# An attention kernel with two MoE layers behind it: a new order for the first two pairs of heads, zero matmuls in five early gaps, K's rounded part by VectorE, and one visit for a pair's product with V

## The chip, the cores and the metric

The kernel runs on one NeuronCore of a Trainium2 chip. The metric is the device time of one execution in microseconds (us). PE is the matmul engine (TensorE), DVE is VectorE, ACT is ScalarE, POOL is GpSimd, and SP is SyncE, which issues all DMAs of this kernel.

## The reference

Inputs are q, k and v of shape (4, 8, 576, 64), a gate s of shape (4, 8, 576), and two pairs of weight matrices (512 x 2048 and 2048 x 512).

```python
def _attn_ref(q, k, v, s):
    scores = scale * np.matmul(q, k.transpose(0, 1, 3, 2))
    cum = np.cumsum(np.maximum(s, 0.0), axis=-1)
    bias = -(cum[:, :, :, None] - cum[:, :, None, :])
    scores = np.where(causal, -1000000000.0, scores + np.minimum(bias, 0.0))
    scores = scores - np.max(scores, axis=-1, keepdims=True)
    attn = np.exp(scores)
    attn = attn / (np.sum(attn, axis=-1, keepdims=True) + 1e-09)
    return np.matmul(attn, v)

def _moe_ref(x, w_in, w_out):
    h = x @ w_in
    return (h - np.tanh(h)) @ w_out

def _moe2_ref(x, w_in, w_out):
    h = x @ w_in
    return (h * np.clip(h + 3.0, 0.0, 6.0) / 6.0) @ w_out

def reference(q, k, v, s, ...):
    x = attention out, transposed to (4 * 576, 8 * 64)
    return _moe2_ref(_moe_ref(x, ...), ...)
```

## The kernel before, in words

The 32 heads are taken as 16 pairs. Every float32 value is kept as a rounded high part (float32r) and a low part, the rest.

For one pair the work is this. SP loads q and k (tile tq). ACT copies the high part of q into Q (`q1`), and POOL subtracts it from q for the low part (`ql`). The high part of K exists twice: one copy beside the row of cumulated gates, for the row maxima (`kh`), and one in the second set of tiles, for the scores (`k2`), from which POOL makes the low part (`kl`). In pairs 0 and 1 `kh` is a cast on DVE and `k2` a copy on ACT. In pairs 2 to 15 `kh` is a copy on ACT, and `k2` is a DMA that copies `kh`'s result from tile K to tile K; the number `KDMA = 2` says from which pair on.

PE then makes one pass of score products just for the row maxima (`mx`, 11 matmuls of 66 rows for a pair), DVE reduces them (`rd`), negates, splits and transposes them (`mf`), and two small DMAs carry them through DRAM into two rows of Q (`mo`, `mi`). After that PE makes the scores themselves (`st`, four chunks a head, 30 matmuls a pair), ACT takes the exponential of each chunk (`ex`), and PE multiplies with V and with a column of ones (`pv`, 128x32 matmuls, 72 + 48 of them). `PVG` says in how many visits PE does this: two visits here, chunks 0 and 1 first, then chunks 2 and 3 and the sums. After the last pair the two MoE layers follow, which are matmuls with conversions of the weights beside them on ACT and DVE.

The order of the instructions on each engine is made by a planner in the kernel file: each operation has an engine, a duration, its predecessors and a priority (table `PRIO`), and a list schedule gives the order in which the program is written down. Each engine then runs its own list in order and waits by semaphores. POOL's operations that share a memory port with DVE are written to wait for the last such DVE operation ahead of them.

Ahead of the first real matmul PE runs 18 matmuls on a tile of zeros (`WARM`, line 1362 of the profile). `FILLS` names operations on PE ahead of which more zero matmuls (128x256, bf16) are put, into a PSUM bank that is idle there; 0.9 stands for 7 of them. Before, there are two such places, ahead of `mx1_0` (the maxima of head 1) and ahead of `st0_0` (the first scores of head 0), 14 matmuls in all.

Before the first pair there is preparation: `cum` (the cumulated gates, on DVE), masks and an identity on POOL (`prep_mask`, `prep_rest`, `prep_ident`), rows of ones in the tiles of pairs 1 to 3 (`prep_first`, two copies on ACT each, lines 369 and 370), and zero columns (`prep_pad`, POOL). The copies of ones are planned as POOL's but run on ACT.

Of the kernel before, what the change touches and what calls it, by code (L numbers as in the profile page):

```python
# [68 lines left out]
KDMA = 2  # L69
# [10 lines left out]
PRIO = {  # L80
# [3 lines left out]
}  # L84
# [170 lines left out]
def vec_us(n, ghz, fixed):  # L255
    return (n / ghz + fixed) / 1e3
# [3 lines left out]
def kernel(  # L260
# [10 lines left out]
    nc = tc.nc  # L271
# [123 lines left out]
    def prep_rest():  # L395
        nc.gpsimd.memset(maskB, 0.0)
        for o in (0, D):
            nc.gpsimd.affine_select(
                out=maskB[o : o + D, 512:S], in_=maskB[o : o + D, 512:S], pattern=[[-1, D]],
                compare_op=ALU.is_ge, fill=-1.0e30, base=0, channel_multiplier=1,  # L400
            )
        for m in zeroed:
            nc.gpsimd.memset(m, 0.0)
        nc.gpsimd.memset(ones, 1.0)
        nc.gpsimd.memset(ones[D:P, 1], 0.0)
# [21 lines left out]
    pr = plan.op("POOL", 1.4, prep_rest, [pma], prio=lead)  # L427
    pid = plan.op("POOL", 1.0, prep_ident, [pr], prio=lead + 1)
    prep = [pf0]
    for i in range(1, NS1):  # L430
        prep.append(plan.op("POOL", 2.6, lambda i=i: prep_first(i), [prep[-1] if i > 1 else pr], prio=lead + i, name=f"ones{i}"))
    pads = []
    for i in range(NS1):
        pads.append(plan.op("POOL", 0.3, lambda i=i: prep_pad(i), [prep[i], prep[0]] + prep[1 : 1 + (i == 0)] + pads[-1:], prio=lead + i + 0.5, name=f"pad{i}"))


# [9 lines left out]
    def heads(p):  # L446
# [6 lines left out]
        al = plan.op("V", 0.0, lambda: None, [alloc_prev[0]] + ([prep[p]] + (pads if p else []) if p < NS1 else []), [b1], t0, name=f"first{p}")  # L453
# [3 lines left out]
        for i, a in enumerate(parts):  # L457
# [23 lines left out]

            act, pool = vec_us(n * S, 1.2, 200), vec_us(n * S, 0.46, 60)
# [7 lines left out]
            oq1.append(plan.op("ACT", act + 0.22 * (p > 0), q1, [lq, al], [b1, tq], t + PRIO["q1"], name=f"q1_{p}"))  # L490
            if p >= KDMA:
                okh.append(plan.op("ACT", act, lambda a=a: nc.scalar.activation(r(b1)[1][0:64, a, 0:S], r(tq)[64:128, a], AF.Copy), [lk, al], [b1, tq], t + PRIO["kh"], name=f"kh{p}"))
                ok2.append(plan.dma(lambda a=a: move(r(b2)[1][64:128, a, 0:S], r(b1)[1][0:64, a, 0:S]), 147 * n, [okh[-1], a2], [b1, b2], t + PRIO["k2"], name=f"k2_{p}"))
            else:
              okh.append(plan.op("DVE", vec_us(n * S, 1.92, 150), kh, [lk, al], [b1, tq], t + PRIO["kh"], name=f"kh{p}", port=True))
              ok2.append(plan.op("ACT", act, k2, [lk, a2], [b2, tq], t + PRIO["k2"], name=f"k2_{p}"))
            oq2.append(plan.dma(q2, 147 * n, [oq1[-1], a2], [b1, b2], t + PRIO["q2"], name=f"q2_{p}"))
            oql.append(plan.op("POOL", pool, ql, [oq1[-1], a2] + first_mf[: p == 1], [b1, b2, tq], t + PRIO["ql"], name=f"ql{p}", port=True))
            okl.append(plan.op("POOL", pool, kl, [ok2[-1]], [b2, tq], t + PRIO["kl"] if p else lead + 3.5 + 0.1 * i, name=f"kl{p}", port=True))
# [15 lines left out]
        for c, (last, kind, tiles) in enumerate(MAXT[p > 0]):  # L515
# [38 lines left out]
            mm_mx[last].append(plan.op("DVE", us, rd, [om, pr, pma], [b, mt], u - PRIO["mx"] + PRIO["rd"], name=f"rd{n}"))  # L554
# [38 lines left out]
        lv = plan.dma(lambda: nc.sync.dma_start(r(vf).rearrange("p j a d -> p (j a d)"), v[p]), 338, first_mo[1:2] if p else first_mo[:1], [vf], t0 + PRIO["lv"], name=f"lv{p}")  # L593
        prep_done.extend(oq1 + okh + oql + okl + oq2 + ok2)
# [56 lines left out]
    def values_of(p, t0, got, vf, lv, xp, xb, bt):  # L651
# [776 lines left out]
```

## Time and profile before

| | us |
|---|---|
| median of three runs | 960.5 (960.0 to 960.62) |
| the profiled execution's own time | 959.44 |
| its span, first to last instruction | 957.6 |
| PE busy | 943.5, 99% of the span |
| DVE, ACT, POOL busy | 653.0, 467.7, 160.0 |
| mean granted clock of PE | 0.978 of full speed |

The attention part ends on PE at about 200 us of the span, the first MoE layer at about 600 us, the second with the end. Busy shares are averages over these parts, so the profile is read part by part. A busy PE need not be a PE at full speed: the granted clock stands beside it.

### The profile page before, as it was taken

What the parts mean: (1) busy time and instruction counts of PE and PEld (TensorE: products, weight loads), DVE (VectorE), ACT (ScalarE), POOL (GpSimd) and SP (SyncE); (2) the same over time, 40 slices, a digit from 0 to 9 for tenths busy, and PEclk for the clock granted to TensorE, in tenths of its full rate; (3) what the DMA queues carried; (4) which work ended last, traced back from release to release, by engine and by line L of the source; (5) the groups of instructions that cost most, each with busy time, mean ns of one, the idle gap of its engine ahead of it and who ended that gap; (6) DMA issues with size and microseconds to landing.
All of it is one profiled execution on the core that took longest, in us unless ns stands there. A gap on an engine that the chain in (4) does not pass through costs nothing.

```text
span 957.6 us, 17848 instructions
## 1 busy us (share of the span) xinstructions
PE 943.5 (99%) x7049; PEld 842.6 (88%) x7049; DVE 653.0 (68%) x1045; ACT 467.7 (49%) x720; POOL 160.0 (17%) x113
## 2 busy tenths in 40 slices
PE   7999999999999999999999999999999999999998
PEld 4787887888888888998888888999999999999997
DVE  5687576868988766775778723656776577764763
ACT  6478685755534443444344333444454444544441
POOL 6445755520000000002322322000000000000000
PEclk7599998999999999999999999999999999999999
DMA  4678988786336447545546681776786767877772
GB/s 113 177 178 217 257 205 230 171 316 196 130 131 220 173 158 267 192 178 199 197 159 242 204 274 38 248 222 208 249 314 222 233 200 256 302 232 223 208 224 98
DMA packets 71424, 197.86 MB, mean 207 GB/s; under 512 B 11696, under 2 KB 20496, under 8 KB 70060
## 3 DMA queue, kind: packets, MB, share of 16 engines
q1 hardware_dynamic: 71340, 196.72, 64.5%
q8 instruction: 55, 0.90, 0.4%
q14 instruction: 29, 0.24, 0.1%
HBM read 143.74 MB, written 44.09 MB: 196 GB/s over the span
## 4 chain that ended last, share of the span: by engine, by line
PE 93%; DVE 2%; DMA 1%; POOL 1%; ACT 1%; SPq 0%; issue 0%; DVEq 0%; POOLq 0%; ACTq 0%
PE bank L927 20%; PE bank L896 20%; PE pair L1264 19%; PE pair L1188 18%; PE bank L627 6%; PE bank L660 5%; PE bank L671 2%; PE bank L526 2%; PE wide L526 1%; DVE xr L535 1%; POOL K L480 1%; DMA tq<-in_k_dram 0%; DMA K<-cdram 0%; POOL Q L470 0%; DMA tq<-in_q_dram 0%
## 5 line engine op out<-in xcount | busy, mean ns | idle before, releaser
L927 PE MATMUL bank<-gg,w 128*128 128x512 f32 (+1 forms) x960 | 234.2, 368 | 0.2 <-ACT gg L915 0.2
L896 PE MATMUL bank<-xx,w 128*128 128x512 f32 (+1 forms) x960 | 233.3, 368 | 0.0
L896 PEld LDWEIGHTS bank<-xx,w 128*128 128x128 f32 x960 | 170.4, 188 | 30.4 <-DVE xx L883 0.2
L927 PEld LDWEIGHTS bank<-gg,w 128*128 128x128 f32 x960 | 170.1, 189 | 30.3 <-ACT gg L915 0.7
L907 ACT ACTIVATE g<-bank 128x512 f32<-128x512 f32 (+1 forms) x80 | 44.5, 556 | 153.1 <-PE bank L896 133.5
L1188 PE MATMUL pair<-op_w,w 128*128 128x384 f32 x648 | 118.0, 334 | 0.6 <-DVE f_w L1208 0.6
L1264 PE MATMUL pair<-w,op_W 128*128 128x256 f32 x918 | 115.1, 283 | 0.0
L1188 PEld LDWEIGHTS pair<-op_w,w 128*128 128x128 f32 x648 | 112.5, 188 | 1.2 <-DVE f_w L1208 0.9
L1264 PEld LDWEIGHTS pair<-w,op_W 128*128 128x128 f32 x918 | 112.8, 192 | 0.0
L917 POOL TENSOR_TENSOR gg<-g,gg 128x512 fp32r<-128x512 f32 x32 | 47.7, 1492 | 344.4 <-ACT gg L915 302.7
L911 DVE TENSOR_TENSOR g<-bank,g 128x512 f32<-128x512 f32 (+1 forms) x80 | 50.8, 636 | 64.7 <-ACT g L907 64.1
L535 DVE CUSTOM_DVE_ANT_0 xr<-bank,xr 128x512 bf16<-128x512 f32 (+3 forms) x96 | 48.9, 509 | 36.3 <-PE bank L526 26.6
L630 ACT ACTIVATE pt<-bank 128x512 f32<-128x512 f32 (+2 forms) x128 | 60.3, 504 | 19.9 <-PE bank L627 15.4
L627 PE MATMUL bank<-Q,K 128*128 128x320 f32 (+9 forms) x384 | 69.1, 326 | 0.6 <-POOL K L480 0.5
L915 ACT ACTIVATE gg<-g 128x512 fp32r<-128x512 f32 (+1 forms) x80 | 46.9, 587 | 40.0 <-DVE g L911 31.7
L627 PEld LDWEIGHTS bank<-Q,K 128*128 128x128 f32 (+3 forms) x384 | 60.0, 197 | 6.0 <-issue 1.6
L660 PE MATMUL bank<-pt,vf 128*32 128x192 f32 (+3 forms) x1152 | 52.0, 330 | 0.0
L470 POOL TENSOR_TENSOR Q<-tq,Q 64x1152 fp32r<-64x1152 f32 (+1 forms) x17 | 43.3, 2548 | 41.6 <-DVE xr L571 13.9
L480 POOL TENSOR_TENSOR K<-tq,K 64x1152 fp32r<-64x1152 f32 (+1 forms) x17 | 43.5, 2560 | 26.3 <-DVE xr L571 9.7
L660 PEld LDWEIGHTS bank<-pt,vf 128*32 128x32 f32 x1152 | 32.5, 114 | 15.1 <-ACT pt L630 3.1
L1264 PE MATMUL pair<-w,op_B 128*128 128x256 f32 x342 | 44.1, 283 | 0.0
L1264 PEld LDWEIGHTS pair<-w,op_B 128*128 128x128 f32 x342 | 42.5, 192 | 0.0
(316 smaller groups left out, 1340.1 us busy)
## 6 DMA issues: line engine op xcount, KB each, us to landing
w<-wdram SPq DMA_DIRECT2D x149, 512.0 KB
wdram<-cv SPq DMA_DIRECT2D x56, 512.0 KB
raw_c<-in_w_dram SPq DMA_DIRECT2D x11, 1024.0 KB
raw_b<-in_w_dram SPq DMA_DIRECT2D x11, 1024.0 KB
raw_a<-in_w_dram SPq DMA_DIRECT2D x12, 512.0 KB
vf<-in_v_dram SPq DMA_DIRECT2D x16, 330.0 KB
rb<-rdram SPq DMA_DIRECT2D x8, 576.0 KB
xdram<-xb SPq DMA_DIRECT2D x16, 288.0 KB
```

The costliest lines, as they stand in the source:

```text
L480: return nc.gpsimd.tensor_sub(x[0:64, a, 0:S], r(tq)[64:128, a], f32(x)[64:128, a, 0:S])
L535: nc.vector.tensor_tensor_reduce(out=junk[0:rr, 0:w], in0=r(b)[0:rr, col : col + w], in1=maskB[:, 0:w] if hh < 0 else maskA[0:rr, m0 : m0 ...
L627: nc.tensor.matmul(o, w, x, start=(i == 0), stop=(i == len(mms) - 1), skip_group_check=True)
L630: nc.scalar.activation(r(pt), r(b)[:, 0 : CW[c]], AF.Exp, scale=0.125)
L660: nc.tensor.matmul(r((wide_b, rest_b)[far])[32 * i : 32 * i + 32, oc : oc + n], r(vf)[:, j, hh, d0 : d0 + 32], r(pts[hh][c])[:, col : col ...
L896: nc.tensor.matmul(r(ps)[:, 0:w], wt[:, c, :], x(c)[:, 0:w], start=(part == 0 and c == 0), stop=(part == 2 and c == NCC - 1),)
L911: nc.vector.tensor_sub(x, r(ps)[:, 0:w], x)
L915: gho = plan.op("ACT", vec_us(w, 1.2, 205), lambda: nc.scalar.activation(r(gh)[:, 0:w], r(g)[:, 0:w], AF.Copy), [m, to_gg], [g, gh], base)
L917: glo = plan.op("DVE" if beside else "POOL", vec_us(w, 0.96, 155) if beside else vec_us(w, 0.44, 160), lambda: (nc.vector if beside else n ...
L927: nc.tensor.matmul(r(acc[e])[:, 0:w], a[:, es], bb[:, 0:w], start=f, stop=l)
L1188: nc.tensor.matmul(bank(k)[:, l], w[hw][:, l, kc], r(x)[:, hx, kc], start=(i in (1, 5, 2) and j == 0 and kc == 0), stop=(j == 2 and kc == ...
L1264: nc.tensor.matmul(r(c[k])[:, m * 256 : (m + 1) * 256], r(x)[:, hx, l, m * P : (m + 1) * P], w[hw][:, l], start=(i == order[chain_first[k] ...
```

## The change

Five things are edited.

1. The preparation is planned anew: the copies of ones are planned as ACT's and come later (pairs 1 and 2 behind pair 0's copies, pair 3 behind pair 1's), and POOL's mask for the last key block and the column of ones move to the end of the preparation (`prep_late`).
2. The table `PRIO` has other numbers, and early operations of pair 0 have fixed early places (`early`). Pair 1's maxima now stand ahead of head 0's scores.
3. `FILLS` names five places: 19 zero matmuls ahead of `mx1_0`, 4 ahead of `mx2_1`, 13 ahead of `st0_0`, 22 ahead of `mx4_1`, 13 ahead of `pv1_3`; 71 in all.
4. `KDMA = ()`: in every pair `kh` is a cast on DVE and `k2` a copy on ACT.
5. `PVG = ((0, 1, 2, 3),)`: all of a pair's product with V in one visit.

```diff
-FILLS = {"mx1_0": 0.9, "st0_0": 0.9}
+FILLS = {"mx1_0": 2.2, "mx2_1": 0.5, "st0_0": 1.6, "mx4_1": 2.6, "pv1_3": 1.6}
-PVG = ((0, 1), (2, 3))
+PVG = ((0, 1, 2, 3),)
-KDMA = 2
+KDMA = ()
...
     def prep_rest():
+        for m in zeroed:
+            nc.gpsimd.memset(m, 0.0)
+
+    def prep_late():
         nc.gpsimd.memset(maskB, 0.0)
...
-    for i in range(1, NS1):
-        prep.append(plan.op("POOL", 2.6, lambda i=i: prep_first(i), [prep[-1] if i > 1 else pr], prio=lead + i, name=f"ones{i}"))
+    def ones_of(i):
+        after = [prep[i // 3], pma, k2s[0]] if i < 3 else [prep[1], k2s[1]]
+        prep.append(plan.op("ACT", 2.4, lambda: prep_first(i), after, prio=lead + 4 + i, name=f"ones{i}"))
...
-            if p >= KDMA:
+            if p in KDMA:
                 okh.append(plan.op("ACT", act, lambda a=a: nc.scalar.activation(r(b1)[1][0:64, a, 0:S], r(tq)[64:128, a], AF.Copy), [lk, al], [b1, tq], t + PRIO["kh"], name=f"kh{p}"))
                 ok2.append(plan.dma(lambda a=a: move(r(b2)[1][64:128, a, 0:S], r(b1)[1][0:64, a, 0:S]), 147 * n, [okh[-1], a2], [b1, b2], t + PRIO["k2"], name=f"k2_{p}"))
             else:
               okh.append(plan.op("DVE", vec_us(n * S, 1.92, 150), kh, [lk, al], [b1, tq], t + PRIO["kh"], name=f"kh{p}", port=True))
-              ok2.append(plan.op("ACT", act, k2, [lk, a2], [b2, tq], t + PRIO["k2"], name=f"k2_{p}"))
+              ok2.append(plan.op("ACT", act, k2, [lk, a2], [b2, tq], early(t + PRIO["k2"], 1.05), name=f"k2_{p}"))
```

What this does to the order is shown at three places. The first is ACT at its start, before. Tiles Q_0 and K_0 belong to pair 0, Q_1, K_1 and Q_2 to pairs 1 and 2; L462 is `q1`, L476 is `k2`, L369 and L370 are the copies of ones.

```order
L423 ACTIVATE rb<-rb 32x576
L462 ACTIVATE Q_0_96<-tq 64x576
L476 ACTIVATE K_0_109<-tq 64x576
L369 ACTIVATE Q_1_99<-Q_0_96 4x1280
L370 ACTIVATE K_1_100<-Q_0_96 4x2x576
L462 ACTIVATE Q_0_96<-tq 64x576
L476 ACTIVATE K_0_109<-tq 64x576
```

The same place of the change; L466 and L480 are now `q1` and `k2`.

```order
L425 ACTIVATE rb<-rb 32x576
L466 ACTIVATE Q_0_96<-tq 64x576
L480 ACTIVATE K_0_109<-tq 64x576
L466 ACTIVATE Q_0_96<-tq 64x576
L480 ACTIVATE K_0_109<-tq 64x576
L369 ACTIVATE Q_1_99<-Q_0_96 4x1280
L370 ACTIVATE K_1_100<-Q_0_96 4x2x576
```

The second half of pair 0's q and k is now copied ahead of the ones. The second place is PE between the maxima of head 1 (K_0, Q_0 into bank_71) and the first scores, before; L526 is `mx`, L1347 a zero matmul and its weights, L627 `st`.

```order
L526 MATMUL bank_71<-K_0_97,Q_0_96 128x128
L1347 LDWEIGHTS xr
L1347 MATMUL bank_72<-xr 128x256
...
L627 MATMUL bank_72<-Q_0_108,K_0_109 128x256
L627 MATMUL bank_72<-Q_0_96,K_0_97 128x256
```

The same place of the change; L531 is `mx`, L1355 a zero matmul, L633 `st`, and K_1, Q_1 are pair 1's.

```order
L531 MATMUL bank_71<-K_0_97,Q_0_96 128x128
L1355 LDWEIGHTS xr
L1355 MATMUL bank_72<-xr 128x256
...
L531 MATMUL bank_72<-K_1_100,Q_1_99 128x512
L531 MATMUL bank_73<-K_1_100,Q_1_99 128x512
...
L1355 MATMUL bank_70<-xr 128x256
...
L633 MATMUL bank_70<-Q_0_108,K_0_109 128x256
```

Pair 1's maxima, eleven matmuls, moved from behind head 0's scores to ahead of them, with 4 zero matmuls ahead of them and 13 behind. The third place is DVE at the end of pair 1's maxima, in the change; L540 is `rd`, L569 to L576 are `mf`, L477 is `kh`, here of pair 2.

```order
L540 ISA xr<-wide,xr 128x384
L540 ISA xr 128x1
L569 COPY xr<-xr 64x1
L572 TENSOR_SCALAR xr<-xr 128x10
L573 SCALAR_TENSOR_TENSOR xr<-xr 128x10
L576 STREAM_TRANSPOSE xr<-xr 128x32
L477 CAST K_2_103<-tq 64x2x576
L540 ISA xr<-bank_65,xr 128x512
```

Before, there is no such cast from pair 2 on; ACT had this copy, and SP a DMA behind it, as these rows of SP show (K_2 is pair 2's, K_0_109 the second tile).

```order
L279 DMA K_0_97<-cdram 2x2x576
L279 DMA K_0_109<-K_2_103 64x2x576
L279 DMA Q_0_108<-Q_2_102 64x2x576
L279 DMA Q_1_99<-mdram 2x40x32
```

The row in the middle with K on both sides is gone from SP's list in the change, in 14 pairs; the cast on DVE is new in 14 pairs, right behind the transpose of the maxima.

## Rows read from the trace of the kernel before

**Rows 1.** The page: granted clock in 40 slices, and the chain by engine.

```profile
PEclk7599998999999999999999999999999999999999
PE 93%; DVE 2%; DMA 1%; POOL 1%; ACT 1%; SPq 0%; issue 0%; DVEq 0%; POOLq 0%; ACTq 0%
```

**Rows 2.** Windows: stretch, length, busy by engine (count), PE clock, DMA share, GB/s.

```profile
10.40:44.54 34.14, 30.18 (x167) 22.75 (x171) 21.41 (x78) 18.97 (x26) 14.30 (x19) 0.50 0.64 164
153.76:160.60 6.84, 6.84 (x40) 5.23 (x42) 2.04 (x8) 3.84 (x7) 6.18 (x3) 0.50 0.54 182
```

**Rows 3.** Timeline of PE at the start: start, length, group, idle before it.

```profile
11.70 1.14 PE L526 MATMUL wide<-K,Q 66*128 66x384 f32 x3 [3.48 <-POOL Q L375]
13.39 1.72 PE L1347 MATMUL bank<-xr 128*128 128x256 bf16 x7
16.73 1.14 PE L526 MATMUL wide<-K,Q 66*128 66x384 f32 x3 [1.62 <-DMA K<-rb]
20.50 0.58 PE L627 MATMUL bank<-Q,K 68*128 68x256 f32 x1 [0.15 <-DMA Q<-mdram]
57.09 1.07 PE L627 MATMUL bank<-Q,K 128*128 128x320 f32 x6
```

**Rows 4.** Timeline of SP's DMA queue at the start.

```profile
4.84 4.11 SPq L279 DMA_DIRECT2D Q<-Q  x2
9.07 1.23 SPq L279 DMA_DIRECT2D K<-rb  x2
```

**Rows 5.** Timeline of ACT at the start.

```profile
4.84 0.68 ACT L476 ACTIVATE K<-tq 64x576 fp32r<-64x576 f32 x1
7.76 0.68 ACT L462 ACTIVATE Q<-tq 64x576 fp32r<-64x576 f32 x1
```

**Rows 6.** Timeline of DVE: maxima of heads 0 and 1, `kh` of pair 1, `mf` of pair 5.

```profile
17.90 0.56 DVE L535 CUSTOM_DVE_ANT_0 xr<-wide,xr 128x384 bf16<-128x384 f32 x1 [1.14 <-PE wide L526]
21.69 0.75 DVE L473 CAST K<-tq 64x1152 fp32r<-64x1152 f32 x1
25.27 0.69 DVE L535 CUSTOM_DVE_ANT_0 xr<-bank,xr 128x512 bf16<-128x512 f32 x1 [2.82 <-PE bank L526]
31.32 0.15 DVE L564 COPY xr<-xr 64x1 f32<-64x1 f32 x1
32.05 0.65 DVE L535 CUSTOM_DVE_ANT_0 xr<-bank,xr 128x512 bf16<-128x512 f32 x1
54.70 1.83 DVE L567 TENSOR_SCALAR xr<-xr 128x10 fp32r<-128x10 f32 x1
```

**Rows 7.** Timeline of PE: a pair at full clock with one visit, to the next pair.

```profile
117.25 0.73 PE L526 MATMUL bank<-K,Q 66*128 66x512 f32 x2
119.16 0.46 PE L627 MATMUL bank<-Q,K 128*128 128x256 f32 x2
123.14 2.92 PE L660 MATMUL bank<-pt,vf 128*32 128x256 f32 x72
127.39 0.73 PE L526 MATMUL bank<-K,Q 66*128 66x512 f32 x2
```

**Rows 8.** The chain that ended last: four product visits of chunks 0 and 1.

```profile
83.29 1.11 PE bank L660 x24
93.78 1.11 PE bank L660 x24
144.67 1.11 PE bank L660 x24
159.39 1.72 PE bank L660 x24
```

**Rows 9.** Waits of 57 to 200 us: who for whom, total, times, longest.

```profile
PE wide L526 <- ACT K L492: 0.7, 1, 0.7
PE bank L627 <- POOL K L480: 0.5, 2, 0.3
```

**Rows 10.** Windows: the sum of six stretches, 48 to 192 us.

```profile
sum 144.00, PE 142.84 PEld 117.16 DVE 104.96 ACT 103.49 POOL 81.65; mean PE 23.81 PEld 19.53 DVE 17.49 ACT 17.25 POOL 13.61
```

More of the change, by code (lines that the diff above doesn't have):

```diff
@@ L401, in prep_rest @@
             )
-        for m in zeroed:
-            nc.gpsimd.memset(m, 0.0)
         nc.gpsimd.memset(ones, 1.0)
@@ L426 @@
     pma = plan.op("POOL", 2.0, prep_mask, prio=lead)
-    pr = plan.op("POOL", 1.4, prep_rest, [pma], prio=lead)
+    pr = plan.op("POOL", 0.4, prep_rest, [pma], prio=lead)
     pid = plan.op("POOL", 1.0, prep_ident, [pr], prio=lead + 1)
-    prep = [pf0]
-    for i in range(1, NS1):
-        prep.append(plan.op("POOL", 2.6, lambda i=i: prep_first(i), [prep[-1] if i > 1 else pr], prio=lead + i, name=f"ones{i}"))
-    pads = []
-    for i in range(NS1):
-        pads.append(plan.op("POOL", 0.3, lambda i=i: prep_pad(i), [prep[i], prep[0]] + prep[1 : 1 + (i == 0)] + pads[-1:], prio=lead + i + 0.5, name=f"pad{i}"))
+    pl = plan.op("POOL", 2.7, prep_late, [pid], prio=lead + 4, name="late")
+    prep, pads, k2s = [pf0], [None], []
+    def ones_of(i):
+        after = [prep[i // 3], pma, k2s[0]] if i < 3 else [prep[1], k2s[1]]
+        prep.append(plan.op("ACT", 2.4, lambda: prep_first(i), after, prio=lead + 4 + i, name=f"ones{i}"))
+        if i == 2:
+            pads[0] = plan.op("POOL", 0.3, lambda: prep_pad(0), [prep[1], prep[2], pl], prio=lead + 5, name="pad0")
+        pads.append(plan.op("POOL", 0.3, lambda: prep_pad(i), [prep[i], pl], prio=lead + 5 + i, name=f"pad{i}"))
     T = PRIO["T"]
@@ L451, in heads @@
         parts = [slice(0, 1), slice(1, 2)] if p == 0 else [slice(0, 2)]
-        al = plan.op("V", 0.0, lambda: None, [alloc_prev[0]] + ([prep[p]] + (pads if p else []) if p < NS1 else []), [b1], t0, name=f"first{p}")
+        al = plan.op("V", 0.0, lambda: None, [alloc_prev[0]] + ([prep[p], pads[p]] if p < NS1 else [pads[0]]), [b1], t0, name=f"first{p}")
         a2 = plan.op("V", 0.0, lambda: None, [alloc_prev[1]], [b2], t0, name=f"second{p}")
@@ L480, in kl @@
                 return nc.gpsimd.tensor_sub(x[0:64, a, 0:S], r(tq)[64:128, a], f32(x)[64:128, a, 0:S])
+            early = (lambda x, y: x if p else lead + y + 0.1 * i)
             act, pool = vec_us(n * S, 1.2, 200), vec_us(n * S, 0.46, 60)
@@ L489, in heads @@
             ) for x in range(2))
-            oq1.append(plan.op("ACT", act + 0.22 * (p > 0), q1, [lq, al], [b1, tq], t + PRIO["q1"], name=f"q1_{p}"))
-            if p >= KDMA:
+            oq1.append(plan.op("ACT", act + 0.22 * (p > 0), q1, [lq, al], [b1, tq], early(t + PRIO["q1"], 1), name=f"q1_{p}"))
+            if p in KDMA:
                 okh.append(plan.op("ACT", act, lambda a=a: nc.scalar.activation(r(b1)[1][0:64, a, 0:S], r(tq)[64:128, a], AF.Copy), [lk, al], [b1, tq], t + PRIO["kh"], name=f"kh{p}"))
@@ L495, in heads @@
               okh.append(plan.op("DVE", vec_us(n * S, 1.92, 150), kh, [lk, al], [b1, tq], t + PRIO["kh"], name=f"kh{p}", port=True))
-              ok2.append(plan.op("ACT", act, k2, [lk, a2], [b2, tq], t + PRIO["k2"], name=f"k2_{p}"))
+              ok2.append(plan.op("ACT", act, k2, [lk, a2], [b2, tq], early(t + PRIO["k2"], 1.05), name=f"k2_{p}"))
             oq2.append(plan.dma(q2, 147 * n, [oq1[-1], a2], [b1, b2], t + PRIO["q2"], name=f"q2_{p}"))
-            oql.append(plan.op("POOL", pool, ql, [oq1[-1], a2] + first_mf[: p == 1], [b1, b2, tq], t + PRIO["ql"], name=f"ql{p}", port=True))
-            okl.append(plan.op("POOL", pool, kl, [ok2[-1]], [b2, tq], t + PRIO["kl"] if p else lead + 3.5 + 0.1 * i, name=f"kl{p}", port=True))
+            oql.append(plan.op("POOL", pool, ql, [oq1[-1], a2] + first_mf[: 2 * (p == 1)], [b1, b2, tq], early(t + PRIO["ql"], 2), name=f"ql{p}", port=True))
+            okl.append(plan.op("POOL", pool, kl, [ok2[-1]] + first_mf[: 2 * (p == 1)], [b2, tq], t + PRIO["kl"] if p else lead + 3.5 + 0.1 * i, name=f"kl{p}", port=True))
         def cu():
@@ L553, in heads @@
                 b.spare = 384
-            mm_mx[last].append(plan.op("DVE", us, rd, [om, pr, pma], [b, mt], u - PRIO["mx"] + PRIO["rd"], name=f"rd{n}"))
+            mm_mx[last].append(plan.op("DVE", us, rd, [om, pr, pma] + [pl] * any(t[0] < 0 for t in tiles), [b, mt], u - PRIO["mx"] + PRIO["rd"], name=f"rd{n}"))
         rd_done.extend(mm_mx[0] + mm_mx[1])
@@ L593, in heads @@
         lv = plan.dma(lambda: nc.sync.dma_start(r(vf).rearrange("p j a d -> p (j a d)"), v[p]), 338, first_mo[1:2] if p else first_mo[:1], [vf], t0 + PRIO["lv"], name=f"lv{p}")
+        k2s.append(ok2[-1])
         prep_done.extend(oq1 + okh + oql + okl + oq2 + ok2)
@@ L680, in values_of @@
             pvs.append(plan.op(
-                "PE", us, lambda cs=cs, last=last: turn_of(cs, last), [g[0][c] for g in got for c in cs] + [lv, pr] + pvs[-1:],
+                "PE", us, lambda cs=cs, last=last: turn_of(cs, last), [g[0][c] for g in got for c in cs] + [lv, pl] + pvs[-1:],
                 [vf, wide_b, rest_b] + [g[1][c] for g in got for c in (range(4) if last else cs)],
@@ L747 @@
     for p in range(NPR):
+        if 0 < p < NS1:
+            ones_of(p)
         heads(p)
```

6 rows, old and new, of the table PRIO are left out of this document.

## The prediction

> **What bounds the kernel now.** I read the page first. The chain that ended last lies on PE for 93% of the span [rows 1], so a change pays only by what it takes from PE's list: idle time, matmul time, or time at a lower clock. The line of the granted clock shows where the last is: 0.7 and 0.5 of full speed in the first two slices of 24 us, one slice of 0.8 later, full speed nearly everywhere else [rows 1]. The windows cut at the edges give two stretches at half speed, the lower of PE's two levels (1.2 against 2.4 GHz): 34.14 us from 10.40, and 6.84 us from 153.76 [rows 2].
>
> PE's timeline at the start shows what came ahead. PE stood idle for 3.48 us up to 11.70 [rows 3], and the clock fell inside that gap. In the 34 us that follow PE is busy for 30.18 [rows 2], yet the clock does not return until the end. The fills that stand there, 7 zero matmuls at 13.39 [rows 3] and as many ahead of the first scores, did not bring it back.
>
> Behind 60 us PE is hardly idle up to the last store, so time won in the attention part should come out at the end, unless DVE, which converts the MoE weights, falls behind.
>
> **The change, part by part.**
>
> *The start.* The wait at 11.70 is put down to POOL [rows 3], but PE's matmul there also waits for the copies of the gate sums into K, which SP issued from 9.07 to 10.30. They stood behind a DMA of Q that held SP's queue until 8.95 [rows 4], because that DMA waits for the second copy of q on ACT, which began at 7.76. ACT's copy before it ended at 5.52 [rows 5]; between them lay the ones of pair 1. In the new order the ones come behind. The copy starts 2.24 us sooner, and SP's list with it: first maxima at 9.46 instead of 11.70, idle 1.24 instead of 3.48. The maxima of head 1 waited for the same kind of DMA [rows 3], behind the same list, and come at 14.49 instead of 16.73.
>
> *The new order with its fills.* I walk it at full clock. A pair costs 1.91 us of maxima (117.25 to 119.16), 3.98 of scores and 4.25 of product in one visit [rows 7]. Seven zeros took 1.72 at half clock [rows 3]: 0.246 each, 0.123 at full. Head 1's maxima (the six like them at 11.70 took 1.69 at half clock [rows 3]; I take 0.95) and 4 zeros run to 15.9, pair 1's maxima to 17.8, 13 zeros to 19.4, head 0's scores to 21.4 (their last rows of Q, through the gap at 20.50 [rows 3], come 2.24 sooner, at 18.3), and 22 zeros to 24.1.
>
> Then PE must wait for DVE, since pair 2's maxima need `kh` of pair 2, and that cast stands behind all of pair 1's maxima. DVE starts head 1 at 17.90 less 2.24, that is 15.66, and needs 3.79 for it with its `mf` (to 21.69). Pair 1 needs 6.05 (25.27 to 31.32), `mf` 0.73, the cast 0.75 [rows 6]. Sum: 26.98. So about 2.9 us behind the 22 zeros PE is idle, and these zeros cost nothing unless they run at half clock.
>
> From 26.98: pair 2's maxima to 28.89, head 1's scores to 30.88, 13 zeros to 32.48, the product to 36.73, pair 3's maxima to 38.64, pair 1's scores to 42.62, pair 4's maxima to 44.53, product to 48.78, and the first chunk of head 4 (0.4) to 49.2. Before, PE got past this same work at 57.09 [rows 3]. **Term 1: 7.9 us.**
>
> *One visit for the product.* Of the pairs behind 57 us, eight do the product in two visits. Two first visits lie 10.49 us apart (83.29 to 93.78 [rows 8]), a pair with one visit takes 10.14 (117.25 to 127.39 [rows 7]): 0.35 a pair. The change waits for a pair's later exponentials inside the visit, where the matmuls of the first chunks cover it. **Term 2: 2.8 us** (lower bound 0.)
>
> *K's high part.* The second low stretch lies between the visits at 144.67 and 159.39 [rows 8]: 14.72 us for a pair that costs 10.49. It began behind a wait of 0.7 us of the maxima for ACT's copy of K [rows 9]. This operation goes to DVE, right behind the transpose, and its DMA goes; the scores twice waited for POOL's low part of K, 0.5 together [rows 9], which stood behind that DMA. **Term 3: 4.2 us** if the clock holds here, 0 if another gap takes the place; **term 4: 0.5.**
>
> *What DVE pays.* Fourteen casts of 0.75 [rows 6] are 10.5 us. In 48 to 192 us DVE is busy for 104.96 of 144 [rows 10], idle for 39. ACT's work stays the same (one copy in place of another), SP loses 14 issues. The upper bound is set by DVE standing behind POOL: a tiny operation on ten columns took 1.83 us, while its like at 31.32 and behind, the whole `mf` of four, took 0.73 [rows 6]. So a cast costs PE between nothing and 0.75 + 1.83 = 2.58. I take 1 us in total, because the idle time is almost four times the casts. The Trainium skill, page "SBUF — State Buffer", section "SBUF: two separate sides", says that DVE in a two-port mode and POOL hold one port pair exclusively for a whole instruction, the loser blocked; the row of 1.83 us agrees. By that rule each cast that meets POOL could wait for the rest of a POOL subtraction, and at worst the 1 us would be 36; that is the rival on DVE below.
>
> *What the clock takes back.* No row shows PE's clock with a gap of 1.24 us behind the 18 zeros, nor with 19 zeros after it. Behind 3.48 us of idle it fell; behind the 0.7 us of rows 9 it fell as well; the gaps of the new order (1.24 ahead of the maxima, 1.7 ahead of head 1's, 2.9 ahead of pair 2's) lie between or near these. So I count on one fall in the first 30 us, with the zeros bringing the clock back before pair 2's maxima: from nothing to the 8.0 worked out below, and I take 3, since the wait for DVE absorbs 2.9 of the delay.
>
> **The sum.** 7.9 + 2.8 + 4.2 + 0.5 = 15.4 won, 1 + 3 given back: 11.4. The profiled execution took 959.44 (span 957.6); the median of the runs is 960.5, 1.06 above it. On the median: 960.5 - 11.4 = 949.1. I predict **949.1 us**. With nothing given back it is 945.1.
>
> **The rivals.**
>
> 1. *The zeros run at half clock and are in the way* (0.19). The fall comes at the first gap and the fills, as the 14 before, do not lift it until those ahead of pair 2. Then, with the other work at most doubled: 9.46 + 1.69 + 4.67 of zeros = 15.8; head 1's maxima 17.5, 4 zeros 18.5, pair 1's maxima 22.3, 13 zeros 25.5, scores 29.5, 22 zeros 34.9, against 26.98: 8.0 us. With 1 for DVE: 954.1. For it speaks that 30.18 us of busy PE did not lift the clock [rows 2], against it that a run of 22 zeros is three times as long as any of the old fills. If it is not lifted before the first product, maxima, scores, 13 zeros and the product add up to 9.8 more, 964.
>
> 2. *DVE becomes the bound* (0.10, on the other side). The place is each pair's cast behind `mf`: if DVE has no room when it comes, everything behind it, the next maxima and with them PSUM banks that PE waits for, comes later by 0.75 to 2.58 a pair. Fully exposed at 2.58 this is 36 us: 948.1 + 36 = 984; at 1.2 a pair it is 965. It decides from 1.0 a pair on (14.3 us over 14 pairs, counted from 948.1, the sum without DVE's 1). For it speak the row of 1.83, against it the 39 us of idle.
>
> 3. *The gain is given back in the first MoE layer* (0.10). DVE carries 10.5 us more while attention is 11 us shorter: of 39 us idle some 17 are left, in pieces. If the weight conversions planned into attention slip behind its end, PE waits for weights there. At two thirds of the gain lost: 957.
>
> 4. *The clock does what it did* (0.06): fall at the first gap, return only with the first product, the second dip again from another gap. Then only the 2.24 us of the start and term 2 remain, less what cold zeros cost: about 959.5, no change that can be told.
>
> **Chances and range.** The forecast has 0.55. A run of this kernel tells about 0.2%, 1.9 us, from no change. Faster holds the forecast, rival 3, and most of rival 1: 0.80. Same: rival 4, a part of 1 and of 2: 0.10. Slower: most of 2 and the tail of 1: 0.10. The low end is everything won with nothing given back, 945.1, less half a microsecond for the 0.95 and 0.4 that I took; the high end is past rivals 1 and 3. Range 944.6 to 958.5, which leaves out rivals 2 and 4 and the tail of 1.
>
> **What would show it.** Right: the first maxima near 9.5 us of the span and head 1's near 14.5; the granted clock of the first two slices at 0.8 or more, and the 128x256 zeros near 0.12 us each; pair 2's maxima at 27 to 30 us, released by DVE; no slice below 0.9 behind 48 us; a pair in 10.1 to 10.3 us; the attention's end on PE near 189 us, not 200. Wrong: zeros at 0.21 us or more, with pair 2's maxima behind 32 us and following a zero matmul without a gap (rival 1); maxima on PE waiting for the cast of K, or casts of over 1.5 us (rival 2); PE idle behind 250 us with ACT or DVE as the releaser of weights (rival 3); a new gap of 0.5 us or more behind 60 us with a low clock after it, which would take term 3 away.

## The result, and the profile after

The changed kernel takes 950.95 us (median of four executions, 948.91 to 952.27), the kernel before in the same comparison 960.56 (960.0 to 962.55): ratio 0.9894, 95% interval 0.9869 to 0.992. The forecast was 949.1. In a second comparison with more executions, on another chip (the run `a_again` below), the changed kernel took 951.07 and the kernel before 956.41: 0.9939, interval 0.9916 to 0.9963. The changed kernel came out alike both times; the kernel before did not. Where it was run 17 to 31 times on a chip, its times fall into two groups, on that second chip 15 of 952.2 to 956.4 us (mean granted clock 0.981 to 0.986) and 14 of 958.3 to 961.9 (0.976 to 0.981). All four executions of the first comparison, and the profiled one, lay in the upper group.

The profiled execution took 952.16 us with a span of 950.4, 7.2 less than the span before. First the page: the granted clock in 40 slices and the chain by engine.

```profile
PEclk8999999999999999999999999999999999999999
PE 95%; DVE 2%; DMA 1%; ACT 1%; POOL 1%; issue 0%; SPq 0%; POOLq 0%; ACTq 0%
```

Where [rows 1] had 7 and 5 the clock now has 8 and 9. The windows show what is left of the low stretches of [rows 2]; the third row reaches from the second chunk of head 4's scores, where PE had got to at 57.09 before [rows 3], to the end of attention.

```profile
15.88:22.30 6.42, 6.42 (x27) 5.13 (x26) 5.50 (x23) 1.87 (x2) 2.60 (x4) 0.50 0.89 220
138.36:145.20 6.84, 6.84 (x65) 4.87 (x68) 5.73 (x18) 4.16 (x6) 6.69 (x4) 0.52 1.02 300
48.76:192.63 143.87, 139.83 (x2222) 117.52 (x2220) 115.91 (x302) 104.99 (x208) 81.83 (x37) 0.98 0.73 193
```

The same part of the kernel before:

```profile
57.09:200.63 143.54, 142.38 (x2223) 116.83 (x2219) 101.73 (x286) 102.39 (x204) 84.44 (x37) 0.98 0.84 218
```

PE has 2.55 us less work in this part after the change, and 2.88 us more idle time (143.87 - 139.83 against 143.54 - 142.38); both have one low stretch of 6.84 us. At the start of this part both kernels have the same work left (2222 and 2223 matmuls counted), so all of the gain of the profiled pair lies ahead of it: 57.09 - 48.76 = 8.33 us. The part behind it is 0.33 longer, and the MoE layers take 757.8 instead of 757.0.

The start, on PE's timeline:

```profile
9.42 0.68 PE L531 MATMUL wide<-K,Q 66*128 66x384 f32 x3 [1.94 <-DMA K<-rb]
10.36 2.25 PE L1355 MATMUL bank<-xr 128*128 128x256 bf16 x19
14.77 0.68 PE L531 MATMUL wide<-K,Q 66*128 66x384 f32 x3 [2.16 <-DMA K<-rb]
19.83 2.94 PE L1355 MATMUL bank<-xr 128*128 128x256 bf16 x13
24.52 2.56 PE L1355 MATMUL bank<-xr 128*128 128x256 bf16 x22
26.84 1.19 PE L531 MATMUL bank<-K,Q 66*128 66x512 f32 x6
48.76 1.04 PE L633 MATMUL bank<-Q,K 128*128 128x320 f32 x6
```

The zeros tell the clock: 19 in 2.25 us is 0.118 each, full speed; 13 in 2.94 is 0.226, half; 22 in 2.56 full again. Pair 2's maxima start at 26.84 with no idle time ahead of them. The cast that they need ended at 26.67, but the 22 zeros, held back by the half clock before them, ran up to the same moment. So this profile can't tell which of the two held the maxima; that of `a_again` below can. DVE's timeline, the last row of a later pair:

```profile
24.38 1.06 DVE L572 TENSOR_SCALAR xr<-xr 128x10 fp32r<-128x10 f32 x1
25.91 0.76 DVE L477 CAST K<-tq 64x1152 fp32r<-64x1152 f32 x1
42.71 0.17 DVE L572 TENSOR_SCALAR xr<-xr 128x10 fp32r<-128x10 f32 x1
```

POOL's timeline beside the first of them:

```profile
20.08 2.61 POOL L474 TENSOR_TENSOR Q<-tq,Q 64x1152 fp32r<-64x1152 f32 x1 [2.83 <-DVE xr L576]
22.77 2.64 POOL L484 TENSOR_TENSOR K<-tq,K 64x1152 fp32r<-64x1152 f32 x1
```

And the second low stretch, which the forecast had counted out. It begins behind a new wait on PE; the chain that ended last goes through a small DMA of 7.14 us there, and SP's queue shows what that DMA stood behind.

```profile
137.56 1.09 PE L531 MATMUL wide<-K,Q 66*128 66x512 f32 x5 [2.09 <-DMA K<-cdram]
```

```profile
127.85 2.44 PE bank L666 x61
130.29 7.14 DMA K<-cdram
```

```profile
128.94 1.29 SPq L736 DMA_DIRECT2D rb<-rdram  x2
130.29 0.45 SPq L279 DMA_DIRECT2D K<-cdram  x1
```

The rows of cumulated gates for pair 13 (2x2x576 numbers) were issued behind two broadcasts of the reciprocals of a token block (64x4x576 each).

### The profile page after: what moved, and what is told of

Same layout as the page of the kernel before. It is cut to its first block, busy times and chain, and to the rows that moved or that the text cites. A ratio compares the mean times of both kernels' runs of the same rounds, so it can differ in the third digit from the quotient of the medians.

```text
span 950.4 us, 17928 instructions
## 1 busy us (share of the span) xinstructions
PE 935.1 (98%) x7106; PEld 841.4 (89%) x7106; DVE 658.3 (69%) x1059; ACT 468.3 (49%) x720; POOL 160.0 (17%) x113
## 4 chain that ended last, share of the span: by engine, by line
PE 95%; DVE 2%; DMA 1%; ACT 1%; POOL 1%; issue 0%; SPq 0%; POOLq 0%; ACTq 0%
PE bank L935 20%; PE bank L904 20%; PE pair L1272 19%; PE pair L1196 18%; PE bank L633 6%; PE bank L666 5%; PE bank L677 2%; PE bank L531 2%; PE wide L531 2%; PE bank L1355 1%; DMA K<-cdram 1%; DMA K<-rb 0%; DVE wy_c L833 0%; DVE w L853 0%; DVE wy_c L831 0%
## 5 line engine op out<-in xcount | busy, mean ns | idle before, releaser
L633 PE MATMUL bank<-Q,K 128*128 128x320 f32 (+9 forms) x384 | 65.4, 311 | 0.3 <-ACT pt L636 0.3
L633 PEld LDWEIGHTS bank<-Q,K 128*128 128x128 f32 (+3 forms) x384 | 56.1, 185 | 6.5 <-issue 2.0
L540 DVE CUSTOM_DVE_ANT_0 xr<-bank,xr 128x512 bf16<-128x512 f32 (+3 forms) x96 | 49.0, 510 | 14.5 <-PE bank L531 3.5
L666 PE MATMUL bank<-pt,vf 128*32 128x192 f32 (+3 forms) x1152 | 48.7, 324 | 0.0
L925 DVE TENSOR_TENSOR gg<-g,gg 128x512 fp32r<-128x512 f32 (+1 forms) x48 | 28.9, 601 | 27.2 <-PE bank L935 25.8
```

The lines of the kernel that those rows point to most:

```text
L540: nc.vector.tensor_tensor_reduce(out=junk[0:rr, 0:w], in0=r(b)[0:rr, col : col + w], in1=maskB[:, 0:w] if hh < 0 else maskA[0:rr, m0 : m0 ...
L633: nc.tensor.matmul(o, w, x, start=(i == 0), stop=(i == len(mms) - 1), skip_group_check=True)
L666: nc.tensor.matmul(r((wide_b, rest_b)[far])[32 * i : 32 * i + 32, oc : oc + n], r(vf)[:, j, hh, d0 : d0 + 32], r(pts[hh][c])[:, col : col ...
L925: glo = plan.op("DVE" if beside else "POOL", vec_us(w, 0.96, 155) if beside else vec_us(w, 0.44, 160), lambda: (nc.vector if beside else n ...
```

## The experiments

All ratios are against the kernel before on the same chip, with a 95% interval. The ratio is the one on record for the comparison and not the quotient of the two medians beside it; the median of a kernel whose times lie in two groups jumps with the share of each. Each profile shows one execution; where that is at an edge of its run's times, its time is given. "Common point" is the start of the second chunk of head 4's scores on PE, 57.09 in the profile of before and 48.76 after; the first chunk stands ahead of it in every version.

**The changed kernel again** (`a_again`).

> The changed kernel unchanged, on the chip of this call, as the measure for the others, since on the chip of the first four runs the kernel before took 955.9 us and not 960.6. If the gain is of the order of the program: 0.989 to 0.992 of the kernel before. If a part of it is chance of where the clock falls: 0.993 to 0.997, with single times spread over 8 us or more in both kernels.

Measured: 951.07 us against 956.41, 0.9939 (0.9916 to 0.9963); single times 947.7 to 954.3. This is the second theory, though the changed kernel's times spread over 6.6 us and not 8. So some 4 of the first 9.6 us lay in the executions, or the chip, on which the kernel before was measured. Its profile, of the slowest of the twelve executions (954.3), has the clock fall elsewhere: PE's timeline, the cast of pair 2 on DVE's, and windows of the stretch at half clock and of the part behind the common point.

```profile
26.68 1.17 PE L531 MATMUL bank<-K,Q 66*128 66x512 f32 x6 [2.47 <-issue]
140.00 1.51 PE L531 MATMUL wide<-K,Q 66*128 66x512 f32 x5 [2.34 <-DMA K<-cdram]
25.82 0.76 DVE L477 CAST K<-tq 64x1152 fp32r<-64x1152 f32 x1
```

```profile
29.50:34.90 5.40, 5.40 (x27) 4.38 (x27) 4.97 (x12) 3.94 (x7) 2.56 (x1) 0.52 0.96 277
51.77:195.05 143.28, 139.53 (x2221) 117.67 (x2220) 114.93 (x305) 104.87 (x208) 81.80 (x37) 0.98 0.73 194
```

The zeros up to the 22 ahead of pair 2's maxima ran at full clock here, PE was done early and stood idle for 2.47 us. The row names no releaser (issue), but the cast ended at 26.58 and the maxima begin 0.10 us later: here they are held by DVE. The fall came after that, where no wait for DVE absorbs it: common point 51.77, 3.0 later than in the other profile. The wait for K's gate rows is there again.

**Without the zeros** (`a_nofill`): the change with

```diff
-FILLS = {"mx1_0": 2.2, "mx2_1": 0.5, "st0_0": 1.6, "mx4_1": 2.6, "pv1_3": 1.6}
+FILLS = {}
```

> The changed kernel without its 71 zero matmuls at the start; order and everything else unchanged. If the zeros bring PE's clock back (the forecast): the clock, which falls at about 16 us, stays at half until the first product or later, so that the common point, 48.76 us with the zeros, comes at 52 to 57 and the time is 954 to 959 us. Rival (zeros in the way or not needed, since PE waits for DVE at pair 2's maxima anyway): the common point at 47 to 49 and 949 to 951 us.

Measured: 953.62 against 955.94, 0.995 (0.9925 to 0.9975). In the profile, of the slowest of the ten executions (958.02; the others took 952.42 to 955.58), the clock stays low for at least 22 us, with long gaps on PE, and the common point comes at 52.72. Timeline and window:

```profile
14.67 1.14 PE L531 MATMUL wide<-K,Q 66*128 66x384 f32 x3 [4.14 <-DMA K<-rb]
52.72 1.04 PE L633 MATMUL bank<-Q,K 128*128 128x320 f32 x6
```

```profile
16.00:38.00 22.00, 18.61 (x107) 14.80 (x109) 18.63 (x56) 10.35 (x18) 8.41 (x7) 0.50 0.75 205
```

The first theory's place of the common point holds in this execution; the median lies just under its 954 to 959. Against `a_again`, on another chip, the zeros are then worth 1 us by the ratios (0.995 and 0.9939) and 2.5 by the medians, at the edge of what these runs tell.

**The ones alone** (`b_ones`): the kernel before with

```diff
-MOVES = []
+MOVES = [("ones1", 0, "k2_0", 1)]
```

> The kernel before with one move on ACT: the copies of the ones of pair 1 come behind the second pieces of head 0, not between them. Theory of the forecast: the first maxima come 2.24 us sooner (9.46 instead of 11.70), but the old fills do not hold the clock, so the low stretch stays until the first product and all of the 2.2 us is at most what comes out: 958 to 959.5 us. Rival (the shorter gap keeps the clock at full): a low stretch much shorter than 34 us and 945 to 954 us. Rival (pair 1 comes later by what head 0 gains): 960 to 961.

(`MOVES` takes an operation out of the finished order and puts it right behind another.) Measured: 953.44 against 955.94, 0.9962 (0.9932 to 0.9991). The first maxima come at 9.45, the common point 2.46 us sooner than before; the low stretch stays, as the first theory has it (its 958 to 959.5 us were counted from the 960.5 of the first comparison). Two rows of PE's timeline, and the granted clock from the page:

```profile
9.45 0.68 PE L526 MATMUL wide<-K,Q 66*128 66x384 f32 x3 [2.45 <-DMA K<-rb]
54.63 1.07 PE L627 MATMUL bank<-Q,K 128*128 128x320 f32 x6
```

```profile
PEclk7699998999999999999999999999999999999999
```

**The zeros alone** (`b_fill`): the kernel before with the change's table `FILLS`.

> The kernel before with the five fills of the change (53 more zero matmuls), order and the rest unchanged. If zeros alone end the first low stretch: 6 to 8 us faster than before, granted clock at full from 30 us on. Rival (they need the new order, since they stand in the way of the work of heads 0 and 1 or come too late): within 2 us of before, the low stretch until the first product.

Four of the five places took zeros in the old order: 58 in all, 44 more than before, where the expectation counted 53. Measured: 952.51 against 956.41, 0.9972 (0.9943 to 1.0001); the median is 3.9 lower, the single times run from 950.1 to 960.09. Windows of the start and of the part behind the common point:

```profile
12.00:32.00 20.00, 17.44 (x107) 13.77 (x106) 13.02 (x48) 11.28 (x15) 9.33 (x10) 0.83 0.73 182
52.06:193.07 141.01, 139.71 (x2223) 114.79 (x2219) 103.17 (x284) 102.16 (x204) 84.66 (x37) 1.00 0.85 222
```

The first low stretch is mostly gone without the new order, with the clock at full from 30 us on, and the common point comes at 52.06, 5.03 sooner. That is the first theory's mechanism without its size: 2.7 us by the ratio and 3.9 by the medians, not 6 to 8, with an interval that just reaches no change. This profile has no second low stretch, so 139.71 is PE's work behind the common point at full clock, with split visits.

**Both** (`b_both`): `b_ones` and `b_fill` together, nothing else of the change.

> The kernel before with two things alone: the copies of the ones of pair 1 behind the second pieces of head 0, and the five fills of the change. The rest of the order, K by ACT and DMA, and the product in two visits stay. Apart they were 2.5 and 3.9 us below the kernel before by medians. If the gain of the change is the start and the zeros alone: 949.5 to 951.5 us, ratio 0.993 to 0.995 as the changed kernel against the kernel before on one chip (0.9939). If the walk's order, K by VectorE or the single visit carry a part: 952.5 to 955 us, ratio 0.996 or above.

Measured: 952.57 against 958.32, 0.9946 (0.9919 to 0.9974). This is the changed kernel's ratio within its interval. The ratio lies in the first theory's range and the time in the second's; the kernel before was slower on this chip than on the one of `a_again`, and no chip ran both this version and the changed kernel. Counted against the kernel before beside it, this version gains 5.8 us by the medians and the changed kernel 5.3; a part of 2 us for the rest of the change, either way, would not show. In the profile (956.03, the second slowest of twelve) the common point comes at 49.01, 8.08 of the 8.33 us that the whole change gained there; then, far behind it, a wait for ACT's copy of K and 12 us at half clock follow.

```profile
49.01 1.07 PE L627 MATMUL bank<-Q,K 128*128 128x320 f32 x6
145.65 1.97 PE L526 MATMUL wide<-K,Q 66*128 66x512 f32 x5 [2.35 <-ACT K L492]
```

```profile
146.00:158.00 12.00, 12.00 (x72) 9.11 (x75) 3.00 (x9) 5.02 (x11) 6.09 (x3) 0.50 0.56 161
```

**One visit alone** (`b_join`): the kernel before, with the first visit moved next to the second in the ten pairs where something stood between them.

```diff
-MOVES = []
+MOVES = [("pv1_0", 0, "mx6_0", 0), ("pv3_0", 0, "st4_0", 0), ("pv5_0", 0, "mx10_4", 0), ...]
```

> The kernel before with the product in one visit in the ten pairs where the maxima or scores of others stand between its two visits; the rest of the order unchanged. Forecast (0.35 us a pair): 2.8 to 3.5 us, 957 to 957.8 us. First rival (the visit's own time, 4.38 split against 4.25 joint): 1.0 to 1.3 us, 959.3. Second rival (the joint visit waits for the late exponentials): 960 to 963, with idle time in front of the product for ACT.

Measured: 957.83 against 955.94, 0.9987 (0.9956 to 1.0018): nothing that can be told, and none of the three theories in its size. The profile, of the fastest of the ten executions (953.53), shows what became of PE's work; window behind the common point, and PE's waits:

```profile
55.49:194.84 139.35, 136.82 (x2223) 115.68 (x2219) 104.50 (x287) 101.69 (x204) 84.54 (x37) 1.00 0.86 225
```

```profile
148.40 1.13 PE L526 MATMUL wide<-K,Q 66*128 66x512 f32 x5 [0.76 <-ACT K L492]
163.69 0.50 PE L627 MATMUL bank<-Q,K 128*128 128x256 f32 x2 [1.41 <-POOL K L480]
```

The same 2223 matmuls at the same clock take 136.82 us of PE's time instead of the 139.71 of `b_fill`: 2.89 less. Eight of the ten joined visits lie in this window (those of pairs 0 and 1 come ahead of the common point), so 0.36 a visit. But PE is idle for 2.53 us instead of 1.30: 1.23 of what is won comes back as waiting, for POOL's low part and ACT's copy of K. Why the other 1.66 does not show in the times is open: six of the ten executions took 957.7 us or more, at mean clocks of 0.977 to 0.98 as in the upper group of the kernel before, and the one trace that was kept is not of these.

**All three** (`b_all`): `b_both` with `b_join`'s moves.

> The kernel before with the three edits of the earlier runs together: ones of pair 1 behind the second pieces of head 0, the fills of the change, and the product in one visit in the ten pairs where it was split. The order's rest and K by ACT and DMA stay as before. If the three add up: common point near 49 us of the span, PE busy near 137 us from there to the end of attention, 948.5 to 951.5 us with a ratio of 0.990 to 0.993, so at or below the changed kernel (0.9939 on one chip). If joined visits only turn PE's time into idle time, or the longer gaps bring a low stretch each: 951.5 to 955 us, ratio 0.994 to 0.998.

Measured: 956.68 against 959.56, 0.9979 (0.9953 to 1.0005). The ratio is the second theory's: the joined visits add nothing to `b_both` that can be told, and with the two intervals overlapping, on two chips, a loss is not shown either. In the profile (958.65, the second slowest of twelve), behind the common point at 51.20, PE is idle for 5.11 us, and the mean clock is 0.95.

```profile
51.20:199.94 148.74, 143.63 (x2223) 119.46 (x2219) 101.70 (x286) 101.58 (x204) 84.65 (x37) 0.95 0.80 211
```

**K by VectorE alone** (`b_k`): the kernel before, order as it was, but in pairs 2 to 15 with

```diff
-okh.append(plan.op("ACT", act, lambda a=a: nc.scalar.activation(r(b1)[1][0:64, a, 0:S], r(tq)[64:128, a], AF.Copy), ...
+okh.append(plan.op("ACT", act, kh, ...          # kh: the cast on DVE
-ok2.append(plan.dma(lambda a=a: move(r(b2)[1][64:128, a, 0:S], r(b1)[1][0:64, a, 0:S]), ...
+ok2.append(plan.dma(k2, ...                     # k2: the copy on ACT
```

(`...` stands for the rest of a line. Cast and copy stand where ACT's copy and the DMA stood in the order, places that were not planned for them; a second edit has POOL's operations wait for these casts as for DVE's others.)

> The kernel before, same order, but K's high part of pairs 2 to 15 made by DVE from what was loaded and its second copy by ACT, as in the change; the 14 DMAs of K are gone. Forecast (terms 3 and 4, less what DVE pays): 3 to 4 us faster than the kernel before, no low stretch near 154 us. Rival (the load of q, late behind the broadcast, sets the wait, whoever copies K): the wait near 151 us stays and the time is within 1 us of the kernel before, the single times in two groups as before.

Measured: 956.67 against 956.41, 1.0007 (0.9982 to 1.0031). That is the rival's time, and a wait near 151 us stays, as the rival has it. The single times, though, are not in two groups: eight of ten lie between 956.29 and 956.92. Window behind the common point, and PE's waits:

```profile
54.99:198.03 143.04, 140.13 (x2223) 114.92 (x2219) 118.79 (x301) 104.67 (x206) 85.85 (x37) 1.00 0.73 194
```

```profile
128.88 0.51 PE L627 MATMUL bank<-Q,K 128*128 128x256 f32 x2 [0.69 <-POOL K L480]
151.70 1.09 PE L526 MATMUL wide<-K,Q 66*128 66x512 f32 x5 [0.91 <-ACT stage L695]
167.73 0.51 PE L627 MATMUL bank<-Q,K 128*128 128x256 f32 x2 [0.74 <-POOL K L480]
```

No low stretch in this part, as the forecast wanted, but the part takes 143.04 us where `b_fill`, with K by ACT and DMA and no low stretch either, takes 141.01. So by one profile of each the cast costs 2.0 us in the old order, 0.42 of it PE's work and 1.61 idle time, and what the missing low stretch saves is paid that way. As the cast stands at a place made for ACT's copy, this is a price in this order and not of the cast as such.

**K by ACT and DMA in the new order** (`a_k`): the change with the two functions of pairs 2 to 15 put back, order as in the change.

> The changed kernel, same order, but K's high part of pairs 2 to 15 made by ACT and its second copy by a DMA from K, as before the change. Forecast (the way of K is what caused the second low stretch): about 4 us slower than the changed kernel, with the scores or maxima waiting for K after 60 us. Rival (the way of K costs nothing of its own): within 1 us of the changed kernel. Other rival (ACT's copy stands at a place in ACT's list made for DVE's and is later): 2 us or more slower, with PE waiting for ACT's copy of K.

Measured: 980.21 against 956.41, 1.0249 (1.0203 to 1.0294). The third theory: 24 us slower. PE's timeline, then ACT's:

```profile
75.97 1.13 PE L531 MATMUL wide<-K,Q 66*128 66x512 f32 x5 [3.42 <-ACT K L500]
```

```profile
74.07 0.66 ACT L826 ACTIVATE wy<-raw_a 128x512 f32<-128x512 f32 x1 [5.69 <-DMA raw_a<-in_w_dram]
74.76 1.16 ACT L500 ACTIVATE K<-tq 64x1152 fp32r<-64x1152 f32 x1
```

ACT's list was made for other work: the copy stands behind a conversion of weights that waits 5.69 us for its load. This tells that this order, made for VectorE's casts, can't take ACT's copy back, and nothing on what the casts are worth in an order made for either way.

**The broadcast, three times.** `a_sp1` and `a_sp2` are the change with the broadcast issued later, `b_sp` the kernel before:

```diff
-MOVES = []
+MOVES = [("sp1", 0, "cu13", 0)]     # a_sp1: behind K's gate rows of pair 13
+MOVES = [("sp1", 0, "lq14", 0)]     # a_sp2: also behind the load of q of pair 14
+MOVES = [("sp1", 0, "lk14", 0)]     # b_sp: behind the loads of q and k of pair 14
```

> The changed kernel with one swap on SP: the gate-sum rows of K for pair 13 are issued ahead of the broadcast of the reciprocals of token block 1 instead of behind it. If the broadcast in front holds up the rows (they took 7.14 us to land): PE's idle 2.09 us at 135.47 and the low clock of 6.8 us behind it vanish, 2 + 3.4 us: 945 to 948 us. Rival (the transfer is late for another reason, or another small transfer behind the broadcast becomes the next wait): the wait only changes its name, idle or low clock of the same size at 136 to 150, 949 to 952 us.

> The changed kernel with the same broadcast issued behind the gate-sum rows of K, the copy of Q and the load of q of pair 14. If a transfer that is late behind the broadcast is what costs time there: no PE idle near 135 us, no low clock at 136 to 148, 947 to 949 us, ratio 0.990 to 0.992. Rival (the swap of the first series, in which the idle time went and the clock still fell, at 128 us: the fall follows short gaps by chance): 950 to 954 us, ratio 0.994 or above, single times over 8 us apart.

> The kernel before with one move on SP: the broadcast of the reciprocals of token block 1 is issued behind the loads of q and k of pair 14, not ahead of them. If this broadcast holds up q and k and with them the maxima at 151 us, whose gap lets the clock fall near 154 in half of the executions: the upper group of times (958 to 962) vanishes, median 953.5 to 955 us, and no wait of the maxima for ACT's copy of K. Rival (the forecast's: ACT's copy itself is what is late): the wait stays, and the times stay in two groups with a median of 955.5 to 957.

Measured: `a_sp1` 954.34 against 955.94, 0.996 (0.9926 to 0.9994), single times from 948.18 to 957.19; `a_sp2` 955.8 against 958.32, 0.9989 (0.9966 to 1.0012); `b_sp` 958.82 against 958.32, 1.0023 (0.9998 to 1.0048). None of the hoped-for times came: `a_sp1` and `b_sp` are slower than both of their theories, `a_sp2` is at its rival's ratio. The wait named went each time: in `a_sp1` and `a_sp2` PE no longer waits for K's gate rows, in `b_sp` not for ACT's copy of K. By itself that shows little for the first two, since PE had run at half clock ahead of these maxima and came to them late, 9.7 us or more behind the issue of the rows. But the trace also records the completion of the rows' DMA: 7.14 us behind its issue in the changed kernel, 1.81 in `a_sp1` and 1.94 in `a_sp2`. So the broadcast did hold up the gate rows, and still no time came of it. PE's timelines of `a_sp1`, `a_sp2` and `b_sp`:

```profile
126.79 0.77 PE L633 MATMUL bank<-Q,K 128*128 128x448 f32 x4 [0.65 <-ACT pt L636]
```

```profile
151.51 0.77 PE L633 MATMUL bank<-Q,K 128*128 128x320 f32 x4 [3.38 <-ACT pt L636]
```

```profile
169.02 0.50 PE L627 MATMUL bank<-Q,K 128*128 128x256 f32 x2 [1.61 <-POOL K L480]
```

In `a_sp2` a wait of 3.38 us for exponentials follows, which the change does not have; in `b_sp` a longer one for POOL. And in `a_sp1` the clock fell ahead of the moved instruction, behind the 0.65 us at 126.79:

```profile
128.00:134.70 6.70, 6.70 (x74) 4.59 (x77) 6.07 (x19) 3.93 (x7) 4.68 (x2) 0.52 0.52 123
```

My theory that this DMA is what costs time there has fallen: without its wait the low stretch is still there in `a_sp1` and `a_sp2`, behind other waits.

## Why the prediction was right

*The start: right.* First maxima at 9.42 (forecast 9.46), head 1's at 14.77 (14.49), behind gaps of 1.94 and 2.16 us where 1.24 and 1.7 were forecast, and the move of the ones alone does it: 9.45 in `b_ones`, 2.46 us at the common point.

*The walk, term 1: right in size, 8.33 against 7.9* (5.32 in `a_again`, where the clock took back 3.0), and with pair 2's maxima at 26.84 (26.98). That DVE's cast holds them is seen in `a_again`, behind 2.47 us of idle time (2.9 forecast); in the first profile the zeros, slowed by the clock, end at the same moment, so that its 26.84 is also chance. What I put down to the new order as a whole is almost all the ones and the zeros: they give 8.08 in the old order (`b_both`).

*Rival 1 did not come:* with the zeros the clock is back after 6.4 us, without them after 22 or more (`a_nofill`), and in the old order they shorten the low stretch too (`b_fill`).

*What the clock takes back, 3 of 0 to 8: inside its range.* It is 0 where the low stretch ends while PE would wait for DVE anyway, and 3.0 where it comes behind that wait (`a_again`); two profiles give no mean.

*Term 2, the single visit: right as work, not as time.* 2.89 us less of PE's time in eight visits (`b_join`), against 2.8 from eight. But a pair took 9.72 to 11.43 us after the change, 10.51 in the mean of seven (visits of the sums from 56.93 to 130.51), not 10.1 to 10.3. The forecast had the waits for late exponentials covered; after the change PE waits 1.5 us for them and 2.1 for the gate rows, with 2.88 us more idle time in all, and in `b_join`, where it waits for POOL's and ACT's work on K instead, 1.23 us come back.

*Term 3, 4.2 us: this step failed*, and by the sign that the prediction named for it, a new gap with a low clock behind it. I put the second low stretch down to ACT's copy of K and let it vanish with that copy. In both profiles of the change a low stretch stands between 138 and 148, behind a wait for another transfer, and attention ends at 192.63, not near 189. In the old order the cast alone gains nothing (`b_k`), and the old stretch is absent from profiles of the old order that still wait for the copy (`b_join`, `b_fill`). So a low stretch in this part is not the price of ACT's copy alone. That copy may have a share in it: in `b_k`, without it, eight of ten executions lie together and the profile has no low stretch there.

*Term 4, 0.5: its cause is not borne out.* The waits for POOL's low part are gone after the change, but `b_k`, which has the DMA removed, waits longer for it, 0.69 and 0.74.

*What DVE pays, 1: too low for the old order,* 2.0 us in `b_k`. In the changed kernel no cast was held: the median of the 17 is 756 ns, the longest 757. The price showed at the operation ahead, the one on ten columns in `mf`. It took 0.17 us in the three pairs where POOL was idle (the row at 42.71), and 0.35 to 1.85 us in the twelve where POOL was running a subtraction, and there it ended 0.03 to 0.04 us behind the end of POOL's (the row at 24.38 ends at 25.44, POOL's low part of K at 25.41). The Trainium skill, page "SBUF — State Buffer", section "SBUF: two separate sides", has DVE and POOL exclude each other on their shared port pair; these rows agree with it. What goes beyond 0.17 adds up to 11.5 us of DVE's time in the changed kernel, against 2.6 in four pairs before and 1.0 in three of `b_k`: it goes with the new order and not with the cast. PE's waits behind the common point name none of it.

*Rivals 2 and 3:* DVE did not become the bound, as PE waits for no cast behind the common point; the MoE layers gave back 0.8 us, where rival 3 had two thirds of the gain.

*The sum.* The profiled pair gained 7.3 us (959.44 - 952.16) where 11.4 were forecast: term 3's 4.2, 2.9 of idle time and 0.8 in the MoE layers are missing, while most of the 4 set aside for DVE and the clock was not called on. The time itself came within 1.9 us of the forecast, and in part that is luck: these misses cancel, and the gain was counted from a kernel before that was in its upper group. Against all its executions on the second chip the change is worth 5.3 us by the medians (6.1 by the means), about half of the 11.4, and about what the ones and the zeros gave alone on another (5.8; 5.3 by the means).

What stays open: why the same short waits are followed by a low clock in one execution and not in the next, and so what makes the two groups of the kernel before; one or two profiles a kernel can't tell. A chip's own part in it looks small on the four chips with many executions: the medians of the kernel before go from 955.9 to 959.6, but its means only from 957.0 to 958.4, and about half of the executions are in the upper group on each. That all of the first comparison's were may be chance or that chip. Also open is what the casts and the single visit would do in an order planned for the change without one of them: no run has that. No version tried has a ratio below the changed kernel's.

## What to carry to other kernels

Before crediting an edit with the end of a low stretch, run the kernel before often enough to see whether it has that stretch every time. Dense zero matmuls in early gaps and one copy moved out of the way of the first transfer gave, within the intervals, as much as a change with five parts; test such small parts alone in the old order first. Work saved on the bounding engine need not come out as time (2.89 us saved in `b_join`, none to be seen): ask which wait ends next.

## What the runs showed of the hardware

- Short waits and the clock: behind 0.65 us of idle time at 126.79 (`a_sp1`) PE ran at half clock for 6.70 us; behind waits of 0.76 and 1.41 us (`b_join`) and 1.61 us (`b_sp`) no window of that part shows it low.
- 34.14 us with 30.18 of busy PE went by at half clock before the change [rows 2]; with 44 zero matmuls more among the same work (`b_fill`) the stretch from 12 to 32 us has a mean of 0.83.
- A DMA of 2x2x576 numbers issued 1.35 us behind a broadcast of two times 64x4x576 landed after 7.14 us; issued ahead of it, after 1.81 (`a_sp1`) and 1.94 (`a_sp2`).
- An operation of DVE on ten columns took 0.17 us with POOL idle and up to 1.85 beside a subtraction on POOL, until that had ended; casts of 0.76 us behind it were not held.
